# Spreading the denominators with 32-row tiles in a four-layer attention and MLP kernel

## The chip, the core and the metric

The kernel runs on one core of a Trainium2 chip. The metric is the device time of one execution in microseconds (us). The core has TensorE (PE in the profile, with its weight loads listed as PEld), VectorE (DVE), ScalarE (ACT), GpSimd (POOL) and SyncE (SP). Each works through its own queue of instructions in order and waits on semaphores for the others. TensorE writes its results to PSUM, which is divided into banks.

## The reference

Four layers run one after the other on x of 2048 rows and 576 columns, in bf16. Layers 1 and 3 are linear attention with 32 heads of 18 columns and share their weights; layers 2 and 4 are an MLP with 4608 hidden columns and share theirs. Each layer normalizes its input and adds its result to it.

```
def _A_ref(x, wqkv, wo):                       # layers 1 and 3
    qkv = x @ wqkv, split into q, k, v of 32 heads x 18
    phi = lambda t: where(t > 0, t + 1, exp(t)) + 1e-6
    pq, pk = phi(q), phi(k)
    kv  = einsum("bhsd,bhse->bhde", pk, v)     # 18 x 18 per head
    z   = einsum("bhsd->bhd", pk)
    num = einsum("bhqd,bhde->bhqe", pq, kv)
    den = einsum("bhqd,bhd->bhq", pq, z) + 1e-6
    return (num / den, heads side by side) @ wo

def _B_ref(x, w1, b1, w2, b2):                 # layers 2 and 4
    return gelu(layernorm(x) @ w1 + b1) @ w2 + b2

x = x + _A_ref(layernorm(x), ...)
x = x + _B_ref(layernorm(x), ...)
x = x + _A_ref(layernorm(x), ...)
x = x + _B_ref(layernorm(x), ...)
```

## The kernel before

Rows are handled in 16 tiles of 128, and tiles in 4 blocks of 512 rows (c is the block, j the tile within it, t = 4c + j). In the code a layer has the number li, from 0: attention is li = 0 and li = 2, called layer 1 and layer 3 here.

**An attention layer.** The first part makes keys, values and query projections and sums up the 18 x 18 matrices. `kv_wo` (L735) then multiplies each of five groups of heads with its rows of wo, so that the output of a row tile is five matmuls (one per group, 126 or 72 rows deep) for each half of the 576 columns. The queries, after phi, lie in tiles `pq[(g, c)]` with one head column per partition (7 heads x 18 = 126 partitions, 72 in group 4) and the 512 rows of the block along the free axis.

**The denominators.** For each block, `den_stage` (L750) has TensorE make the denominators of all 32 heads: for each of four column blocks of 128 rows, 32 heads on 32 partitions, in one PSUM tile of 128 x 128. ScalarE turns them into reciprocals as exp(-ln(den)), in the tile `rden`. They now have to be spread over the 18 columns of each head. `quad_stage` (L769) has VectorE place the four 32-partition strips of `rden` as a block diagonal into a 128 x 512 tile `quad_rden`, with a mask. `scale_stage` (L779), once per group, has TensorE multiply the selection matrix `head_bc[:, g, :]` with it (one matmul of 512 columns, 128 deep, L784), ScalarE copy the result out of PSUM to `rden_bc` (L788) and VectorE multiply `pq` with it in place (L789). With `direct=True` the copy is left out and VectorE reads PSUM.

**The output loop** runs over t from 0 to 15 (L834). `wo_stage(t)` (L793) is ten matmuls into one of two PSUM tiles, accA or accB by turns; `residual` (L504) adds the old row tile on VectorE and stores the sum to `x_d` through SP. In between come the work of the next block (its five scale stages after tiles 0 and 1 of this block, the den stage of the block after next after tile 1) and what is left of the query projections. The old row tiles come from `prefetch_xo` (L486): pairs straight from the input in layer 1, and row tiles from `x_d` in layer 3. They share the pool `rows`, nine tiles, with the sums; a tile is free again when its last reader or store is done. `AHEAD` is 4.

**The next layer's normalization.** `lnp` (L301) is a pipeline whose items move by one step on each `tick`: statistics, rstd, mean times rstd, normalized rows, transposes on TensorE with a copy to `yT`. In the output loop it takes the first four row tiles for the MLP; `hold` is the number of ticks that an item waits first, `tp_at` the tile t from which its transposes may go. Statistics are made on VectorE, or, with `stats="act"`, by two passes on ScalarE that are put behind the last reciprocal.

**PSUM.** The pool `ps_h` has four banks, used in turn by query projections (until phi has read them on ScalarE), den stages, scale stages and transposes. `ps_acc` holds accA and accB of two banks each.

**Order.** Within the attention layers and the MLP, `pe()` chains TensorE's instructions in the order of the code. On the other engines a planner orders instructions when the kernel is built, by the order of the code and by when it reckons that they are ready; dependencies of the kind NOSYNC (`tc.add_manual_dep`) force an order where they stand.

**The start.** All first loads go through SP in one chain (`chained`): row tiles 0 and 1, the key part of wqkv, row tile 2, the value part, and so on. ScalarE loads its table of functions at once.

Of the kernel before, what the change touches and what calls it, by code (L numbers as in the profile page):

```python
# [8 lines left out]
ALU = mybir.AluOpType  # L9
BF16 = mybir.dt.bfloat16  # L10
F32 = mybir.dt.float32
# [4 lines left out]
P = 128  # L16
NT = S // P
# [11 lines left out]
CA = 512  # L29
NCA = S // CA  # L30
# [4 lines left out]
def build(tc, A_x, A_wqkv, A_wo, B_w1, B_b1, B_w2, B_b2, out, dbg=None, n_layers=4):  # L35
    nc = tc.nc
    dbg = dbg or {}
    with ExitStack() as ctx:
        const = ctx.enter_context(tc.tile_pool(name="const", bufs=1))
        ps_h = ctx.enter_context(tc.tile_pool(name="ps_h", bufs=4, space=PSUM))  # L40
# [3 lines left out]
        x_in = A_x.flatten_outer_dims()  # L44
# [14 lines left out]
        head_bc = const.tile([P, G, P], BF16, name="head_bc")  # L59
# [49 lines left out]
        AHEAD = 4  # L109
        turned = const.tile([P, D // 32, TPC, 32], BF16, name="turned")  # L110
# [6 lines left out]
        rows = ctx.enter_context(tc.tile_pool(name="rows", bufs=9))  # L117
# [6 lines left out]
        NOSYNC = mybir.DependencyInfo(mybir.DependencyClass.NoSync, mybir.DependencyReason.SCHED_ONLY)  # L124
# [3 lines left out]
        chain = dict(last=None)  # L128

        def chained(inst):  # L130
            if chain["last"] is not None:
                tc.add_manual_dep(inst.ins, chain["last"], NOSYNC, reason="start-up DMA issue order")
            chain["last"] = inst.ins.name
            return inst
# [3 lines left out]
        def pe(inst):  # L138
            if pe_chain["on"]:
                if pe_chain["last"] is not None:  # L140
                    tc.add_manual_dep(inst.ins, pe_chain["last"], NOSYNC, reason="TensorE order in the MLP")
                pe_chain["last"] = inst.ins.name
            return inst

        def load_x0(t):
            x0 = blk.tile([P, D], BF16, name="x0", tag="blk")
            chained(nc.sync.dma_start(out=x0[:], in_=x_in[t * P:(t + 1) * P, :]))
            x0_tiles[t] = x0

        def load_wqkv(part):  # L150
# [3 lines left out]
            chained(nc.sync.dma_start(out=wqkv_sb[0:64, 4, cols], in_=A_wqkv[4 * P:D, cols]))  # L154

        load_x0(0)
        load_x0(1)
        load_wqkv(1)
        load_x0(2)
        load_wqkv(2)  # L160
        load_x0(3)
        load_x0(4)
# [10 lines left out]
                pe(nc.tensor.matmul(warm_ps[:], lhsT=y_ring[NY - 1][:, 0:P], rhs=y_ring[NY - 1][:, 0:512],  # L173
                                    start=True, stop=True))

        nc.scalar.preload_act_table_set("natural_log_exp_and_others")
        nc.vector.memset(wqkv_sb[64:P, 4, :], 0.0)
        for vr in v_ring:
            nc.gpsimd.memset(vr[:, 4, 72:126], 0.0)
# [40 lines left out]
        dve_last = dict(norm=None, sum=None, phi=None)  # L220
# [223 lines left out]
        lnp = LNPipe()  # L444
# [41 lines left out]
        def prefetch_xo(li, t, add_b2):  # L486
            if li == 0:
                if t % 2 == 0:
                    pair = rows.tile([P, 2, D], BF16, name="xo_pair", tag="row")
                    chained(nc.sync.dma_start(  # L490
                        out=pair[:], in_=x_in[t * P:(t + 2) * P, :].rearrange("(two p) d -> p two d", two=2)))
                    for i in range(2):
                        xo_of[(li, t + i)] = pair[:, i, :]
                return
            xo = row_tile("xo")
            load = nc.sync.dma_start(out=xo[:], in_=x_d[t])
            if not add_b2:
                behind(load, "landed")
            if add_b2:
                tc.add_manual_dep(load.ins, dve_last["sum"], NOSYNC, reason="no residual rows ahead of their stage")  # L500
                nc.gpsimd.tensor_tensor(out=xo[:], in0=xo[:], in1=b2_bc[:], op=ALU.add)  # L501
            xo_of[(li, t)] = xo[:]
# [25 lines left out]
        def layer_A(li, next_kind, pre_a1=None):  # L528
# [217 lines left out]

            quad_rden = {}
            rden_of = {}

            def den_stage(c, after=None, pair=None):  # L750
                if pair:
                    dp = ps_acc.tile([P, 2, 512], F32, name="den_pair", tag=pair)[:, 0, :]
                else:
                    dp = ps_h.tile([P, 512], F32, name="den_ps", tag="h")
                for g in range(G):
                    rows = 127 if g == 0 else GR[g]
                    for j in range(TPC):
                        pe(nc.tensor.matmul(dp[32 * j:32 * (j + 1), 0:P], lhsT=zsel[0:rows, g, :],
                                         rhs=pq[(g, c)][0:rows, j * P:(j + 1) * P],
                                         start=(g == 0), stop=(g == G - 1)))  # L760
                rden = work.tile([P, P], BF16, name="rden", bufs=1)
                log = nc.scalar.activation(out=dp[:, P:2 * P], in_=dp[:, 0:P], func=ACT.Ln)
                if after is not None:
                    tc.add_manual_dep(log.ins, after, NOSYNC, reason="copies first")
                act_last["rden"] = nc.scalar.activation(out=rden[:], in_=dp[:, P:2 * P], func=ACT.Exp,
                                                        scale=-1.0).ins.name
                rden_of[c] = rden

            def quad_stage(c, after=None):  # L769
                quad = blk.tile([P, D], BF16, name="quad_rden", tag="blk")  # L770
                spread_out = nc.vector.tensor_tensor(
                    out=quad[:, 0:CA].rearrange("p (j n) -> p j n", j=4), in0=quad_mask[:],
                    in1=rden_of.pop(c)[:].unsqueeze(1).to_broadcast([P, 4, P]), op=ALU.mult)
                if after is not None:
                    tc.add_manual_dep(spread_out.ins, after, NOSYNC, reason="sums first")
                quad_rden[c] = quad
                dve_last["quad"] = spread_out.ins.name

            def scale_stage(g, c, pair=None, direct=False):  # L779
                if pair:  # L780
                    bp = ps_acc.tile([P, 2, 512], F32, name="rden_pair", tag=pair)[:, 0, :]
                else:
                    bp = ps_h.tile([P, 512], F32, name="rden_ps", tag="h")
                pe(nc.tensor.matmul(bp[:, 0:CA], lhsT=head_bc[:, g, :], rhs=quad_rden[c][:, 0:CA], start=True, stop=True))  # L784
                spread_rows = bp
                if not direct:
                    spread_rows = blk.tile([P, D], BF16, name="rden_bc", tag="blk")
                    act_last["copy"] = nc.scalar.copy(out=spread_rows[0:GR[g], 0:CA], in_=bp[0:GR[g], :]).ins.name  # L788
                mult = nc.vector.tensor_tensor(out=pq[(g, c)][0:GR[g], 0:CA], in0=pq[(g, c)][0:GR[g], 0:CA],  # L789
                                               in1=spread_rows[0:GR[g], 0:CA], op=ALU.mult)  # L790
                dve_last["mult"] = mult.ins.name

            def wo_stage(t):  # L793
                c, j = divmod(t, TPC)
                wp = ps_acc.tile([P, 2, 512], F32, name="wo_ps", tag=("accA", "accB")[t % 2])
                for half in range(2):
                    for g in range(G):
                        pe(nc.tensor.matmul(wp[:, half, 0:HALF], lhsT=pq[(g, c)][0:GR[g], j * P:(j + 1) * P],  # L798
                                              rhs=kvwo[g][0:GR[g], half * HALF:(half + 1) * HALF],
                                              start=(g == 0), stop=(g == G - 1)))  # L800
                xn = residual(li, t, wp[:, :, 0:HALF])
                if xn is not None and next_kind == "B" and t < TPC:
                    lnp.feed(xn, t, "B", "pool", "act", hold=(2, 2, 6, 6)[t], tp_at=6 + 2 * t,
                             **(dict(after="sum") if t % 2 else dict(stats="act", after="rden")))

            for t in range(AHEAD):
                prefetch_xo(li, t, add_b2=False)
            if "b1" in bias_stage:
                bias_casts()
# [12 lines left out]
            if li == 0:  # L822
                late = [q_proj(*q_left.pop(0), defer=True)]
            for g in range(3):
                scale_stage(g, 0)
            kv_wo(4)
            scale_stage(3, 0, pair="accA")
            late.append(q_proj(*q_left.pop(0), defer=True))
# [4 lines left out]
                phi(after=act_last["rden"])  # L833
            for t in range(NT):  # L834
                c, j = divmod(t, TPC)
                if t + AHEAD < NT:
                    prefetch_xo(li, t + AHEAD, add_b2=False)
                wo_stage(t)
                for late in list(rden_of):
                    quad_stage(late, after=dve_last["sum"])  # L840
                if q_left:
                    q_proj(*q_left.pop(0))
                if c + 1 < NCA:
                    for g in ((0, 1, 2), (3, 4), (), ())[j]:
                        scale_stage(g, c + 1)
                if j == 1 and c + 2 < NCA:
                    den_stage(c + 2)
                if t == NT - 3:
                    warm_table(ACT.Gelu_apprx_tanh, act_last["copy"])
                state["wo"] = t  # L850
                lnp.tick()
                if t < 10:
                    lnp.tick(transposes=0)
# [237 lines left out]
```

## Time and profile before

| | |
|---|---|
| median of 3 runs | 766.43 us (766.31 to 766.50) |
| the profiled execution | 766.11 us, of which its span is 764.4 us |
| granted TensorE clock | 1.000 |
| TensorE busy | 758.8 us, 6522 matmuls |
| ScalarE, VectorE, GpSimd busy | 336.5, 271.6, 123.4 us |
| layer 1, output stage | about 77 to 106 us of the span |
| layer 3, output stage | about 453 to 479 us of the span |

The profile is of one execution. Its times run from the first instruction. In a line of the timeline stand the start, the length, the engine, the line of the code (L784), the operation, what it writes and reads, the shapes, the number of instructions merged (x3), and in brackets the idle time of that engine just before, with what ended it. Groups carry busy time, mean ns of one, and idle time before. SPq is SyncE's queue of transfers.

### The profile page before, as it was taken

What the parts mean: (1) busy time and instruction counts of PE and PEld (TensorE: products, weight loads), DVE (VectorE), ACT (ScalarE), POOL (GpSimd) and SP (SyncE); (2) the same over time, 40 slices, a digit from 0 to 9 for tenths busy, and PEclk for the clock granted to TensorE, in tenths of its full rate; (3) what the DMA queues carried; (4) which work ended last, traced back from release to release, by engine and by line L of the source; (5) the groups of instructions that cost most, each with busy time, mean ns of one, the idle gap of its engine ahead of it and who ended that gap; (6) DMA issues with size and microseconds to landing.
All of it is one profiled execution on the core that took longest, in us unless ns stands there. A gap on an engine that the chain in (4) does not pass through costs nothing.

```text
span 764.4 us, 15650 instructions
## 1 busy us (share of the span) xinstructions
PE 758.8 (99%) x6522; PEld 492.1 (64%) x6522; DVE 271.6 (36%) x684; ACT 336.5 (44%) x751; POOL 123.4 (16%) x198
## 2 busy tenths in 40 slices
PE   8999999999999999999999999999999999999998
PEld 6776664675477457646777767447745764674476
DVE  7785963135113603400355678600240032000000
ACT  5888856304710650164056577570064036205600
POOL 4681222012000301200110004200020021001000
PEclk9999999999999999999999999999999999999999
DMA  9992473016401721330246007530231033011000
GB/s 262 270 299 49 158 275 85 17 47 178 110 24 63 203 62 42 97 85 1 75 120 215 1 16 245 206 81 17 62 105 41 16 125 81 9 32 55 2 9 24
DMA packets 80289, 73.82 MB, mean 97 GB/s; under 512 B 36698, under 2 KB 64858, under 8 KB 80218
## 3 DMA queue, kind: packets, MB, share of 16 engines
q1 hardware_dynamic: 80218, 72.82, 32.6%
q8 instruction: 51, 0.84, 0.5%
q14 instruction: 20, 0.16, 0.1%
HBM read 48.03 MB, written 24.77 MB: 95 GB/s over the span
## 4 chain that ended last, share of the span: by engine, by line
PE 98%; DVE 1%; DMA 1%; ACT 0%; SPq 0%; issue 0%
PE m_ps L972 36%; PE h_ps L914 20%; PE hp_ps L914 16%; PE q_ps L588 5%; PE wo_ps L798 5%; PE k_ps L540 3%; PE k_ps L612 3%; PE k_ps L629 2%; PE v_ps L561 1%; PE m_half L972 1%; PE v_ps L558 1%; PE rden_ps L784 1%; PE tp L423 1%; DMA wqkv_sb<-in_A_wqkv_dram 1%; PE kvacc L582 1%; PE k_tail L629 1%
## 5 line engine op out<-in xcount | busy, mean ns | idle before, releaser
L972 PE MATMUL m_ps<-w_sb,hT 128*128 128x288 bf16 x2232 | 274.8, 286 | 0.0
L972 PEld LDWEIGHTS <-hT 128*128 128x128 bf16 x2304 | 224.8, 98 | 59.8 <-issue 3.4
L914 PEld LDWEIGHTS <-w_sb 64*128 64x128 bf16 x2304 | 124.5, 94 | 136.5 <-issue 1.9
L914 PE MATMUL hp_ps<-yT,w_sb 64*128 64x512 bf16 x1152 | 178.0, 376 | 0.0
L914 PE MATMUL h_ps<-yT,w_sb 64*128 64x512 bf16 x1152 | 148.0, 376 | 0.0
L919 ACT COPY relay_sb<-relay_sb 128x1 f32<-128x1 f32 x144 | 28.6, 198 | 262.3 <-PE h_ps L914 220.0
L910 ACT ACTIVATE hT<-h_ps,b1T 128x512 bf16<-128x512 f32 x144 | 91.2, 684 | 44.4 <-PE h_ps L914 44.4
L374 POOL TENSOR_TENSOR ln_rstd<-ln_u,neg_half 128x1 f32<-128x1 f32 x64 | 36.6, 574 | 370.8 <-DVE ln_u L365 226.4
L910 ACT ACTIVATE hT<-hp_ps,b1T 128x512 bf16<-128x512 f32 x144 | 91.2, 693 | 0.0
L518 DVE TENSOR_TENSOR xbf<-m_ps,xo 128x576 bf16<-128x576 f32 x15 | 11.4, 757 | 212.9 <-PE m_ps L972 212.9
L518 DVE TENSOR_TENSOR xo<-m_ps,xo 128x576 f32<-128x576 f32 x16 | 12.1, 758 | 176.1 <-PE m_ps L972 176.1
L501 POOL TENSOR_TENSOR xo<-xo,b_bc 128x576 f32<-128x576 f32 x32 | 41.0, 1287 | 100.4 <-DMA xo<-x_d 63.7
L914 PE MATMUL h_ps<-yT,w_tail 64*128 64x512 bf16 x144 | 54.1, 376 | 0.0
L914 PE MATMUL hp_ps<-yT,w_tail 64*128 64x512 bf16 x144 | 54.1, 376 | 0.0
L588 PE MATMUL q_ps<-yT,wqkv_sb 128*126 128x512 bf16 (+1 forms) x200 | 49.8, 380 | 0.0
L798 PE MATMUL wo_ps<-kvwo,pq 126*128 126x288 bf16 (+1 forms) x320 | 43.3, 286 | 0.5 <-DVE pq L789 0.5
L914 PEld LDWEIGHTS <-w_tail 64*128 64x128 bf16 x288 | 27.1, 94 | 17.1
L798 PEld LDWEIGHTS <-pq 126*128 126x128 bf16 (+1 forms) x320 | 30.1, 97 | 10.5 <-DVE pq L789 1.0
L467 ACT ACTIVATE phi_e<-k_ps 128x288 bf16<-128x288 f32 x46 | 19.3, 419 | 38.8 <-PE k_ps L612 35.8
L588 PEld LDWEIGHTS <-wqkv_sb 128*126 128x126 bf16 (+1 forms) x200 | 24.9, 131 | 11.4 <-issue 0.2
L475 DVE TENSOR_SCALAR phi_e<-phi_e 128x288 bf16<-128x288 bf16 (+2 forms) x86 | 24.7, 288 | 20.1 <-ACT phi_e L467 19.4
L467 ACT ACTIVATE phi_e<-q_ps 126x512 bf16<-126x512 f32 (+1 forms) x40 | 23.8, 596 | 18.0 <-PE q_ps L588 18.0
(136 smaller groups left out, 657.0 us busy)
## 6 DMA issues: line engine op xcount, KB each, us to landing
xo<-x_d SPq DMA_DIRECT2D x48, 288.0 KB
x_d<-xo SPq DMA_DIRECT2D x32, 288.0 KB
xl<-x_d SPq DMA_DIRECT2D x24, 288.0 KB
y_d<-turned SPq DMA_DIRECT2D x40, 144.0 KB
w_sb<-in_B_w_dram SPq DMA_DIRECT2D x6, 864.0 KB
yT<-y_d SPq DMA_DIRECT2D x10, 512.0 KB
w_sb<-in_B_w_dram SPq DMA_DIRECT2D x9, 512.0 KB
x_d<-xn SPq DMA_DIRECT2D x16, 288.0 KB
```

Of the source, the lines that this page charges most:

```text
L374: nc.gpsimd.tensor_tensor(out=rstd[:], in0=it["u"][:], in1=neg_half[:], op=ALU.pow)
L467: exp = nc.scalar.activation(out=e_out, in_=ps_ap, func=ACT.Exp)
L475: low = nc.vector.tensor_scalar(out=e[0:rows, 0:n], in0=e[0:rows, 0:n], scalar1=1.0, scalar2=1e-6, op0=ALU.min, op1=ALU.add)
L501: nc.gpsimd.tensor_tensor(out=xo[:], in0=xo[:], in1=b2_bc[:], op=ALU.add)
L518: total = nc.vector.tensor_tensor(out=xn[:, cols].rearrange("p (h n) -> p h n", h=2), in0=halves, in1=xo[:, cols].rearrange("p (h n) -> p ...
L588: pe(nc.tensor.matmul(qp[0:GR[g], :], lhsT=wqkv_sb[:, k, GO[g]:GO[g] + GR[g]], rhs=yT[:, k, c * CA:(c + 1) * CA], start=(k == 0), stop=(k ...
L629: pe(nc.tensor.matmul(dst, lhsT=lhsT, rhs=pk, start=(t == 0), stop=(t == NT - 1)))
L798: pe(nc.tensor.matmul(wp[:, half, 0:HALF], lhsT=pq[(g, c)][0:GR[g], j * P:(j + 1) * P], rhs=kvwo[g][0:GR[g], half * HALF:(half + 1) * HALF ...
L910: act_last["gelu"] = nc.scalar.activation(out=to, in_=ps, func=ACT.Gelu_apprx_tanh, bias=b1T[:, f:f + 1], scale=1.0).ins.name
L914: mm = pe(nc.tensor.matmul(dst[n], lhsT=wt, rhs=mv, start=(seen[n] == 0), stop=(seen[n] == 8)))
L919: relay = nc.scalar.copy(out=relay_sb[:, 1:2], in_=relay_sb[:, 0:1])
L972: pe(nc.tensor.matmul(acc[half][:, 0:HALF], lhsT=hT[f][:, j * P:(j + 1) * P], rhs=w2_sb[:, f, half * HALF:(half + 1) * HALF], start=(f == ...
```

## The change

In both attention layers the spread of blocks 1 to 3 is made another way. `quarter_stage(c)` needs no block diagonal for groups 0 to 3: for each group and each 32-partition strip i of `rden` it makes one matmul 32 rows deep, 126 wide, of 128 columns, which fits in a 32-row tile of the array. The four strips write four different PSUM banks, all of `ps_h`, each of which in the end holds the four groups of one strip. ScalarE copies the four banks to `turned`, a tile that otherwise serves to turn rows in the MLP, and `quarter_scale` has VectorE multiply the four groups from there. Group 4 still goes by `quad_stage` and `scale_stage`, and so does block 0.

The steps stand at other places in the loop: for block 1, the quarter stage comes after tile 1 and the products after tile 2; for block 2, the quarter stage comes after tile 3 and the products after tiles 4 and 5, and for block 3 after tile 7 and after tiles 8 and 9. Group 4 of block 1 is spread after tile 2, that of blocks 2 and 3 after tiles 4 and 8. The den stage of block 2 moves to tile 2. Query projections that are left go after tiles 0 and 2. Layer 3 asks for six residual row tiles before the loop instead of four. Layer 1's group 0 of block 0 is multiplied straight from PSUM. The normalization items get other holds and transposition times and change statistics engines (even tiles on VectorE, odd ones on ScalarE). At the start, row tiles 1 and 2 are loaded through ScalarE's queue, ahead of its table.

```diff
-        def load_x0(t):
+        def load_x0(t, by_act=False):
             x0 = blk.tile([P, D], BF16, name="x0", tag="blk")
-            chained(nc.sync.dma_start(out=x0[:], in_=x_in[t * P:(t + 1) * P, :]))
+            if by_act:
+                chain["act"] = nc.scalar.dma_start(out=x0[:], in_=x_in[t * P:(t + 1) * P, :]).ins.name
+            else:
+                chained(nc.sync.dma_start(out=x0[:], in_=x_in[t * P:(t + 1) * P, :]))
...
-        load_x0(1)
+        load_x0(1, by_act=True)
         load_wqkv(1)
-        load_x0(2)
+        load_x0(2, by_act=True)
...
-        nc.scalar.preload_act_table_set("natural_log_exp_and_others")
+        load = nc.scalar.preload_act_table_set("natural_log_exp_and_others")
+        tc.add_manual_dep(load.ins, chain["act"], NOSYNC, reason="first rows first")
...
+            def quarter_stage(c):
+                rden = rden_now["tile"]
+                banks = [ps_h.tile([P, 512], F32, name="rden_ps", tag="h") for _ in range(4)]
+                for g in range(4):
+                    for i in range(4):
+                        rows = slice(32 * i, 32 * (i + 1))
+                        pe(nc.tensor.matmul(banks[i][0:126, g * P:(g + 1) * P], lhsT=head_bc[rows, g, 0:126],
+                                            rhs=rden[rows, :], start=True, stop=True))
+                spread_rows = turned[:].rearrange("p a t c -> p (a t c)").rearrange("p (i w) -> p i w", i=4)
+                for i in range(4):
+                    act_last["copy"] = nc.scalar.copy(out=spread_rows[0:126, i, 0:4 * P], in_=banks[i][0:126, :]).ins.name
+
+            def quarter_scale(c, groups, after):
+                spread_rows = turned[:].rearrange("p a t c -> p (a t c)").rearrange("p (i w) -> p i w", i=4)
+                for g in groups:
+                    scaled = pq[(g, c)][0:126, 0:CA].rearrange("p (i n) -> p i n", i=4)
+                    mult = nc.vector.tensor_tensor(out=scaled, in0=scaled,
+                                                   in1=spread_rows[0:126, :, g * P:(g + 1) * P], op=ALU.mult)
+                    tc.add_manual_dep(mult.ins, after, NOSYNC, reason="sums first")
+                    dve_last["mult"] = mult.ins.name
...
-                    lnp.feed(xn, t, "B", "pool", "act", hold=(2, 2, 6, 6)[t], tp_at=6 + 2 * t,
-                             **(dict(after="sum") if t % 2 else dict(stats="act", after="rden")))
-
-            for t in range(AHEAD):
+                    lnp.feed(xn, t, "B", "pool", "act", hold=(2, 2, 2, 4)[t] if li > 0 else (2, 8, 8, 10)[t], tp_at=6 + 2 * t if li > 0 else (6, 10, 11, 14)[t],
+                             **(dict(after="sum") if t % 2 == 0 else dict(stats="act", after="rden")))
+
+            for t in range(AHEAD if li == 0 else AHEAD + 2):
                 prefetch_xo(li, t, add_b2=False)
...
             for g in range(3):
-                scale_stage(g, 0)
+                scale_stage(g, 0, direct=(li == 0 and g == 0))
...
             for t in range(NT):
                 c, j = divmod(t, TPC)
-                if t + AHEAD < NT:
-                    prefetch_xo(li, t + AHEAD, add_b2=False)
+                if li == 0 and t + AHEAD < NT or 0 < t < NT - AHEAD - 1 and li > 0:
+                    prefetch_xo(li, t + AHEAD + (li > 0), add_b2=False)
                 wo_stage(t)
-                for late in list(rden_of):
-                    quad_stage(late, after=dve_last["sum"])
-                if q_left:
+                total = dve_last["sum"]
+                if c + 1 < NCA:
+                    for g in ((), (), (0, 1, 2, 3), ())[j] if c == 0 else ((0, 1), (2, 3), (), ())[j]:
+                        quarter_scale(c + 1, (g,), after=total)
+                    if t == 1:
+                        quarter_stage(1)
+                    if j == 3 and c + 2 < NCA:
+                        quarter_stage(c + 2)
+                    if j == (2 if c == 0 else 0):
+                        scale_stage(4, c + 1)
+                if j == (2 if c == 0 else 1) and c + 2 < NCA:
+                    den_stage(c + 2)
+                    if c > 0:
+                        quad_stage(c + 2, after=total)
+                if t == 3:
+                    quad_stage(2, after=total)
+                if q_left and t in (0, 2):
                     q_proj(*q_left.pop(0))
-                if c + 1 < NCA:
-                    for g in ((0, 1, 2), (3, 4), (), ())[j]:
-                        scale_stage(g, c + 1)
-                if j == 1 and c + 2 < NCA:
-                    den_stage(c + 2)
+                    if t == 2:
+                        q_proj(*q_left.pop(0))
```

## The prediction

> **What bounds the kernel now.** All times are in us. I read the page first: busy time and the chain of work that ended last.
>
> ```profile
> PE 758.8 (99%) x6522; PEld 492.1 (64%) x6522; DVE 271.6 (36%) x684; ACT 336.5 (44%) x751; POOL 123.4 (16%) x198
> ...
> PE 98%; DVE 1%; DMA 1%; ACT 0%; SPq 0%; issue 0%
> ```
>
> TensorE is the bound, so an edit counts only if it removes TensorE work, removes one of its few waits, or adds a wait. Next the TensorE timeline of layer 1's output stage (start, length; lengths overlap, so work is read from start to start).
>
> ```profile
> 77.08 0.67 PE L798 MATMUL wo_ps<-kvwo,pq 126*128 126x288 bf16 x4
> 78.02 0.91 PE L798 MATMUL wo_ps<-kvwo,pq 72*128 72x288 bf16 x6 [0.28 <-DVE pq L789]
> ...
> 82.81 0.59 PE L784 MATMUL rden_ps<-quad_rden,head_bc 128*128 128x512 bf16 x2
> 83.34 0.47 PE L758 MATMUL den_ps<-pq,zsel 127*32 127x128 bf16 x20
> 83.74 1.40 PE L798 MATMUL wo_ps<-kvwo,pq 126*128 126x288 bf16 x10
> ```
>
> Three things are read here. A wo tile costs 1.23 (ten matmuls). A spread matmul (L784) costs 0.216. The den stage, whose 20 matmuls go four abreast in 32-column tiles, occupies 83.74 - (82.81 + 2 x 0.216) = 0.50, and its single starts in the trace show why: 0.093 lost entering the tiled form, five steps of 0.045 to 0.057, 0.097 lost leaving. Then the one real wait, at layer 1's entry, on the engines that feed it:
>
> ```profile
> 74.64 1.57 ACT L788 CAST rden_bc<-rden_ps 126x512 bf16<-126x512 f32 x3
> 75.28 0.42 DVE L789 TENSOR_TENSOR pq<-pq,rden_bc 126x512 bf16<-126x512 bf16 x1 [1.13 <-ACT rden_bc L788]
> 75.62 0.75 DVE L743 CAST kvwo<-kvwo_ps 72x576 bf16<-72x576 f32 x1
> 76.28 1.08 DVE L789 TENSOR_TENSOR pq<-pq,rden_bc 126x512 bf16<-126x512 bf16 x3
> 77.29 0.68 DVE L789 TENSOR_TENSOR pq<-pq,rden_ps 72x512 bf16<-72x512 bf16 x1
> ```
>
> VectorE sat idle 1.13 for ScalarE's first copy; its last product ends at 77.97 and TensorE goes on at 78.02. The start of the kernel:
>
> ```profile
> 0.80 0.86 SPq L147 DMA_DIRECT2D x<-in_A_x_dram  x2
> 1.71 0.43 SPq L152 DMA_DIRECT2D wqkv_sb<-in_A_wqkv_dram  x1
> 5.80 0.48 ACT L426 COPY yT<-tp 128x384 bf16<-128x384 bf16 x1 [3.72 <-PE tp L423]
> 6.92 0.77 PE L540 MATMUL k_ps<-wqkv_sb,yT 128*128 128x288 bf16 x5 [0.61 <-DMA wqkv_sb<-in_A_wqkv_dram]
> ```
>
> **First loads.** Each issue holds SP for 0.43 to 0.47. With row tile 1 moved to ScalarE's queue, the key weights are issued 0.47 earlier (1.24 for 1.71). Against it, row tiles 0 to 2 (144 KB each) now land beside them; at the page's 262 GB/s one is 0.55. The first projection can start no earlier than the yT copy's end, 6.28. So the gain is between -0.1 and 0.6; I take 0.3, nearer the issue time, since the trace's packets are sparse around 3 to 4 us. On ScalarE two issues (0.9) go ahead of the table load (1.28, from 0.79): it ends near 3.0, before the first copy at 5.80. TensorE has no wait over 0.04 between 8.6 and 66, so the gain is carried on.
>
> **Layer 1's entry.** Group 0's product now reads PSUM: 0.68 on VectorE instead of 0.42, but it can start when the spread ends (74.44), not at 75.28. ScalarE loses one copy (0.48). The four later products then end about 0.5 earlier, and TensorE's 0.44 before 78.02 shrinks to under 0.1. A wait of 0.12 before the query projection at 75.29, for a bank that the copy frees, goes too. Gain 0.5; bounds 0.2 and 0.57. What is late next is TensorE itself.
>
> **The quarter spread.** For blocks 1 to 3 of each layer, four spread matmuls (4 x 0.216 = 0.864) become sixteen of 128 columns, four abreast in 32-row tiles. No row shows 32-row tiles. The nearest is the den stage: the same two changes of form (0.19) and steps of four 128-column matmuls; here four steps, not five. Its weights are 32 wide, these 126; a 126-wide load in L649 of layer 3 holds a 0.057 step:
>
> ```profile
> 447.32 0.96 PE L649 MATMUL kv_ps<-k,wqkv_sb 128*126 128x126 bf16 x15
> ```
>
> So 0.19 + 4 x 0.057 = 0.42, and I take 0.45, as a first wide load after a change of form costs up to 0.05 more in that stage (0.105 for 0.057). The ends are 0.35 (part of the change hidden) and 1.10 (loads one by one). Saving 0.41 x 6 = 2.5. By the Trainium skill, TensorE: Matmul & The Clock Gate, Measured speedup vs the span model, 4x row packing was measured at 3.07 times; by that the four steps would take 0.864 / 3.07 = 0.28 (an estimate) instead of 0.23 and the sum would be 0.3 smaller; no run here shows it yet.
>
> ScalarE still makes four copies and VectorE four products per block, of the same sizes:
>
> ```profile
> L788 ACT CAST rden_bc<-rden_ps 126x512 bf16<-126x512 f32 x30 | 15.9, 597 | 5.2 <-PE rden_ps L784 5.2
> L789 DVE TENSOR_TENSOR pq<-pq,rden_bc 126x512 bf16<-126x512 bf16 x32 | 13.3, 437 | 1.9 <-ACT rden_bc L788 1.3
> ```
>
> **The new wait.** The quarter stage takes all four banks of ps_h, so its first four matmuls wait for the last user of each, and everything behind in TensorE's order waits too. I laid the stage out by those rows' cadences (ScalarE 0.48 a pass, VectorE 0.33 a product and 0.66 a sum); the same layout of the kernel before ends each layer within 0.15 of the trace. Layer 1: block 1 is ready at about 80.5, but the last query tile's second pass ends near 80.66, 0.14; block 2 the same, behind two projections, 0.14; block 3 waits for a yT copy behind statistics on ScalarE, 0.23. Layer 3: 0.14, 0.05 and 0.23. There the group 4 spread of block 2, 1.23 (one wo tile) after the quarter stage, must get a bank back, while ScalarE has a row's two statistics passes (0.80 + 0.78) and the first copy (0.60) to do: 0.4. Together 1.3; ends 0.6 and 2.1.
>
> **Edits at nothing.** The residual tiles: the trace has nine loads issued in one go already,
>
> ```profile
> 404.67 4.96 SPq L496 DMA_DIRECT2D xo<-x_d  x9
> ```
>
> as many as the row pool has tiles, so loading six ahead instead of four moves none. Later loads wait for a tile on SP with the stores x_d behind; their cover is time (the tenth tile's load goes out at 463.4, its sum starts at 471.1). If that is gone, VectorE's sum waits and, two tiles on, TensorE; the nearest row is the one sum in the list of waits that waited 1.0 for such a load. The statistics that change engine and place lie beside TensorE. Layer 1's last transposes move to t = 14, so their copy (0.44 + 0.72) has wo 15 and the switch to cover it (0.28 + 1.23): 0.3 to spare, and up to 0.3 if ScalarE is late.
>
> **Sum.** 0.3 + 0.5 + 2.5 - 1.3 = 2.0. The profiled execution took 766.11 (span 764.4 and 1.7 around it), so its like is 764.1; it lay 0.32 below the median 766.43, so I forecast 764.4. A run tells a change of about 0.2% (1.5 us) from none.
>
> **Rivals.**
> 1. The waits eat the saving: statistics passes are put ahead of the copies in both layers, so the third quarter stage of layer 1 waits 1.0 and not 0.23, and layer 3 loses another 0.5 in waits at wo 4 and at the next spread. For it: the statistics at 92.26 in the trace run ahead of a yT copy whose transpose had long ended. Against: these holds were moved, so the order may be another. Gain about 0.7: 765.7. Chance 0.22.
> 2. Slower: the sixteen weight loads go one after another. Then a step is 4 x 0.057, the stage 0.91 + 0.19 = 1.10, each of six loses 0.24 (1.4), and with waits of about 0.9 the sum is 0.3 + 0.5 - 1.4 - 0.9, 1.5 slower: 767.9. It decides from a stage of about 0.78 on. For it: no row here has four wide loads within one step. Against: L914's two 64-row loads start 0.004 apart and their matmuls run in pairs. Chance 0.12. The Trainium skill speaks for this one in part: LDWEIGHTS (loading the stationary operand), on the same page, has a load's time set by its columns, so that 32 rows cost as much as 128, and its 126 / 1.2 = 105 ns (an estimate) would make it dearer still; the 0.057 steps of L649 are against that figure.
> 3. The banks come free in time: waits of 0.3 and a stage of 0.40 give 0.3 + 0.5 + 2.8 - 0.3 = 3.3 faster: 763.1. Chance 0.08.
>
> **How the numbers follow.** The forecast's case has the remaining 0.58; its own range, from first loads (-0.3 to +0.3) and waits (0.6 to 2.1), is 763.2 to 765.5, and about a tenth of the chance lies above 764.9, the 0.2% mark. So faster: 0.47 + 0.08 = 0.55. Rival 2 straddles the mark on the other side (767.96), and a shortage of row tiles could add to it: slower 0.10. The rest is 0.35. The range 762.7 to 766.6 holds the forecast and rivals 1 and 3 with their bounds and leaves out rival 2.
>
> **What would show it.** Right: 96 matmuls of 32 rows, L784 down from 40 to 16, each quarter stage 0.40 to 0.50 from start to start; the wait before 78.02 gone; k_ps starting near 6.6; TensorE waits of 0.05 to 0.4 ahead of the quarter stages, released by ScalarE. Wrong: quarter stages near 1.1, or waits of 1 us in the output stages, or VectorE sums waiting for xo loads.

## The result and the profile after

| | before | after |
|---|---|---|
| median | 766.46 us (766.31 to 766.72, 6 runs) | 771.29 us (771.09 to 773.13, 6 runs) |
| ratio | | 1.0066, 95% interval 1.0056 to 1.0077 |
| profiled execution | 766.11, span 764.4 | 773.13, span 771.4 |
| granted TensorE clock | 1.000 | 0.995 |

The change makes the kernel 4.8 us slower; the forecast was 764.4, or 2.0 faster. The profile of after is of the slowest of its six executions; it lies 1.8 above the others. It loses 1.79 at the start, which only some executions do, as the runs on the first loads below show; that the other five are quicker there and nowhere else was not profiled. All times below are in us.

The page of after, busy time, chain, and the group of wo matmuls:

```profile
PE 761.1 (99%) x6594; PEld 492.7 (64%) x6594; DVE 271.4 (35%) x684; ACT 335.9 (44%) x750; POOL 125.2 (16%) x198
PE 95%; DVE 2%; DMA 1%; issue 0%; ACT 0%; SPq 0%; POOL 0%; DVEq 0%; ACTq 0%
L826 PE MATMUL wo_ps<-kvwo,pq 126*128 126x288 bf16 (+1 forms) x320 | 45.5, 291 | 4.9 <-DVE xo L522 4.8
```

TensorE's busy time should have fallen by the spread that went, and it is 2.3 longer; its share of the chain fell from 98% to 95%; and wo now waits 4.8 for VectorE's sums. In TensorE's timeline of layer 1, the parts that were forecast are there:

```profile
78.79 1.48 PE L826 MATMUL wo_ps<-kvwo,pq 126*128 126x288 bf16 x10
...
82.51 0.45 PE L806 MATMUL rden_ps<-rden,head_bc 32*126 32x128 bf16 x16
82.89 0.91 PE L826 MATMUL wo_ps<-kvwo,pq 126*128 126x288 bf16 x6
```

The ten wo matmuls at layer 1's entry run through without the wait of 0.44, and the quarter stage takes 0.38 from its first start to the next wo, with 0.096 lost ahead of it: 0.475, in all six places.

The account, by starts of TensorE's stages in the two profiles: the start loses 1.79 (den_ps of block 0 at 73.83 instead of 72.04), layer 1 from there to its first h_ps gains 1.57 (32.37 for 33.94), layer 2 and layer 3's first part change by nothing (the first den_ps of layer 3 comes at 447.15 instead of 446.93, the 0.22 that the first two leave), the output stage of layer 3 from its first wo to the MLP's first h_ps loses 5.62 (32.27 for 26.65), and what follows loses 1.18 (286.20 for 285.02).

The loss in layer 3 starts on SP. The list of its waits, for the load of a residual row tile (line L500 in after):

```profile
SPq L500 <- DMA x_d<-xo: 6.6, 3, 5.0
SPq L500 <- POOL y_ring L395: 4.6, 2, 3.3
```

(us in total, times, longest; in before the same two read 2.8, 3, 1.4 and 2.3, 1, 2.3.) Then the timeline of layer 3, in order:

```profile
466.36 1.82 POOL L395 TENSOR_SCALAR y_ring<-xo,ln_rstd,ln_nmr 128x576 bf16<-128x576 f32 x1
468.21 0.32 SPq L500 DMA_DIRECT2D xo<-x_d  x1
468.63 0.85 SPq L529 DMA_DIRECT2D x_d<-xo  x2
474.55 0.32 SPq L500 DMA_DIRECT2D xo<-x_d  x1
...
477.71 0.76 DVE L522 TENSOR_TENSOR xo<-wo_ps,xo 128x576 f32<-128x576 f32 x1 [2.75 <-DMA xo<-x_d]
478.53 1.39 PE L826 MATMUL wo_ps<-kvwo,pq 126*128 126x288 bf16 x10 [1.66 <-DVE xo L522]
...
481.92 1.48 DVE L522 TENSOR_TENSOR xo<-wo_ps,xo 128x576 f32<-128x576 f32 x2 [3.44 <-DMA xo<-x_d]
482.73 2.56 PE L826 MATMUL wo_ps<-kvwo,pq 126*128 126x288 bf16 x10 [2.81 <-DVE xo L522]
```

The load of row tile 11 is to go into the buffer of row tile 2, which GpSimd is still normalizing until 468.18; SP waits for it with that load at the head. Behind it in SP's queue stand the stores of sums 4 and 5; sum 4 was done by 464.4, but its store goes out at 468.63; sum 5 was done at 466.48, its store goes at 469.06. The load of row tile 12 is to go into the buffer of row tile 4, so it waits until that store has landed, at 474.53. In before the planner had the buffers in another order: the load of row tile 11 went into row tile 4's, behind that store (464.67), and did not wait for GpSimd. The loads of row tiles 11, 12 and 15 there, and the last three row tiles on TensorE:

```profile
467.81 0.32 SPq L496 DMA_DIRECT2D xo<-x_d  x1
...
470.09 0.32 SPq L496 DMA_DIRECT2D xo<-x_d  x1
...
473.96 0.45 SPq L496 DMA_DIRECT2D xo<-x_d  x1
...
475.58 3.86 PE L798 MATMUL wo_ps<-kvwo,pq 126*128 126x288 bf16 x30
```

So in before the loads of row tiles 12 to 15 had gone out at 470.09 to 473.96; after the change they go at 474.55 to 478.36, and the transfers then take 3.0 to 6.1 to land among the others. Sums 12 and 13 wait 2.75 and 3.44 for their rows, and TensorE, two PSUM tiles on, 1.82 and 2.98 (by its starts). What it does next is at half speed, as the table by stretches shows (the columns are length, busy time of each engine with its instructions, granted clock, DMA share, GB/s):

```profile
470.00:476.00 6.00, 6.00 (x58) 4.85 (x56) 4.42 (x9) 3.92 (x7) 0.98 (x2) 1.00 0.46 138
476.00:482.00 6.00, 2.26 (x18) 1.52 (x16) 0.84 (x2) 0.37 (x1) 0.00 (x0) 0.90 0.96 307
482.00:488.00 6.00, 5.27 (x26) 2.35 (x27) 2.16 (x3) 0.19 (x1) 0.00 (x0) 0.53 1.04 398
```

The granted clock is 0.53 in the last row, and wo matmuls go at steps of 0.240 instead of 0.122. The DMA share of 0.46 in the first row shows the stalled queue: in before it was 0.88 in the same stretch.

```profile
470.00:476.00 6.00, 6.00 (x55) 4.69 (x53) 4.67 (x9) 4.65 (x9) 2.23 (x4) 1.00 0.88 308
```

### The profile page after: what moved, and what is told of

It reads as the page before. It is cut to its first block, busy times and chain, and to the rows that moved or that the text cites. A ratio compares the mean times of both kernels' runs of the same rounds, so it can differ in the third digit from the quotient of the medians.

```text
span 771.4 us, 15788 instructions
## 1 busy us (share of the span) xinstructions
PE 761.1 (99%) x6594; PEld 492.7 (64%) x6594; DVE 271.4 (35%) x684; ACT 335.9 (44%) x750; POOL 125.2 (16%) x198
## 4 chain that ended last, share of the span: by engine, by line
PE 95%; DVE 2%; DMA 1%; issue 0%; ACT 0%; SPq 0%; POOL 0%; DVEq 0%; ACTq 0%
PE m_ps L1011 36%; PE h_ps L953 20%; PE hp_ps L953 16%; PE q_ps L592 6%; PE wo_ps L826 4%; PE k_ps L616 3%; PE k_ps L544 2%; PE k_ps L633 2%; PE v_ps L565 1%; PE m_half L1011 1%; PE v_ps L562 1%; PE tp L427 1%; DMA xo<-x_d 1%; DVE xo L522 1%; PE k_tail L633 1%; PE kvacc L586 1%
## 5 line engine op out<-in xcount | busy, mean ns | idle before, releaser
L826 PE MATMUL wo_ps<-kvwo,pq 126*128 126x288 bf16 (+1 forms) x320 | 45.5, 291 | 4.9 <-DVE xo L522 4.8
```

## The experiments

Theory A: the order on SP costs the time in layer 3. The first four runs set it against the six tiles ahead (B), the quarter spread or the normalization on other engines (C) and the shorter holds by themselves (D).

**Four tiles ahead.** The diff is against after.

```diff
-            for t in range(AHEAD if li == 0 else AHEAD + 2):
+            for t in range(AHEAD):
...
-                if li == 0 and t + AHEAD < NT or 0 < t < NT - AHEAD - 1 and li > 0:
-                    prefetch_xo(li, t + AHEAD + (li > 0), add_b2=False)
+                if t + AHEAD < NT:
+                    prefetch_xo(li, t + AHEAD, add_b2=False)
```

> After, with the residual tiles of layer 3 asked for as before (four at the entry, then one four tiles on at each row tile) instead of six and five on. Theory A (the queue order of layer 3 costs the time, and six or four tiles make no difference to it, since nine loads go out in one go in either): as after, 771.0 to 771.6, VectorE's sums waiting 2.7 and 3.4 for loads again. Theory B (asking two tiles further ahead fills the nine row tiles too early): the waits of layer 3 go, 764.5 to 766. The start's share: if den_ps of block 0 comes at 72.0 in this profile rather than at 73.8, the 1.8 that the profiled run of after lost at the start is chance of that run; if it is 73.8 again, it belongs to the change.

Measured: 770.57 (769.26 to 771.93, 4 runs), ratio 1.0054 (1.0039 to 1.0069). The program that is built from it has the same instructions in the same order on every engine as after: the planner sends nine loads out at once either way. So B falls, and the run is a second profile of after. In it TensorE waits 0.94 and 2.20 for late sums, and layer 3's output stage takes 29.87 where the first profile has 32.27, so the loss there differs between executions. den_ps of block 0 comes at 72.35: the 1.8 at the start is not in every execution.

**Stores first.** One order is added on SP; the order of the other four engines stays as in after.

```diff
+        last_store = {}
...
                 behind(load, "landed")
+                if t >= 9:
+                    tc.add_manual_dep(load.ins, last_store["ins"], NOSYNC, reason="stores first")
...
-            nc.sync.dma_start(out=x_d[t], in_=xn)
+            store = nc.sync.dma_start(out=x_d[t], in_=xn)
+            last_store["ins"] = store.ins.name
```

> After, with each residual load of layer 3 from the tenth tile on held in SP's order behind the store of the row tile summed before it; no other engine's order changes. Theory A (a load that waits on SP for POOL's normalization of row tile 2 keeps the stores of sums 4 and 5 behind it, and the next load takes the tile whose store was kept): the waits of VectorE's sums for loads (2.75 and 3.44) fall under 1.2 each, TensorE's 4.8 ahead of wo and the half-speed stretch behind them go, layer 3 ends at least as early as before: 764.3 to 766.0. Theory C (layer 3's quarter spread or its normalization on the other engines costs the time, and SP only follows): SP's stores go out earlier but TensorE's waits stay, 770 to 771.5.

Measured: 764.53 (764.36 to 766.06, 10 runs), ratio 0.9976 (0.9966 to 0.9985): 6.8 below after (6.0 below the same program in the run with four ahead) and 1.9 below before. SP's part of its timeline:

```profile
467.63 0.42 SPq L501 DMA_DIRECT2D xo<-x_d  x1
468.15 0.43 SPq L532 DMA_DIRECT2D x_d<-xo  x1
468.68 0.89 SPq L501 DMA_DIRECT2D xo<-x_d  x1
```

and TensorE's:

```profile
474.04 3.86 PE L830 MATMUL wo_ps<-kvwo,pq 126*128 126x288 bf16 x30
477.83 1.04 PE L957 MATMUL h_ps<-yT,w_sb 64*128 64x512 bf16 x8
```

The load of row tile 11 waits for GpSimd as in after (it goes out at 466.77, and all of this profile lies 1.44 earlier). But the store of sum 4 has gone out at 462.98, as the sum ended, so the load of row tile 12 follows at 467.63, where after has it at 474.55; the last load is out by 473.2, and thirty wo matmuls follow each other with no wait into the MLP. The output stage of layer 3 takes 26.32 instead of 32.27, and the granted clock is 1.00 throughout it. The loads of row tiles 11 and 12 take the same buffers as in after; nothing but the place of the loads in one queue was changed, so A is shown and C falls.

**Layer 3's normalization as before.**

```diff
-                    lnp.feed(xn, t, "B", "pool", "act", hold=(2, 2, 2, 4)[t] if li > 0 else (2, 8, 8, 10)[t], ...
-                             **(dict(after="sum") if t % 2 == 0 else dict(stats="act", after="rden")))
+                    lnp.feed(xn, t, "B", "pool", "act", hold=(2, 2, 6, 6)[t] if li > 0 else (2, 8, 8, 10)[t], ...
+                             **(dict(after="sum") if t % 2 == (li > 0) else dict(stats="act", after="rden")))
```

> After, with the normalization behind layer 3 as before: holds 2, 2, 6, 6 and ScalarE's statistics on row tiles 0 and 2 turned back to 1 and 3 as they were. Theory A: the order that the planner gives SP then has the stores of sums 4 and 5 ahead of the load that waits, so the time falls as in the run with stores first, 764.3 to 766.0. Theory C as the quarter spread itself: no change, 770 to 771.5. Theory D (the shorter holds bring POOL's and ScalarE's work against the sums, whatever SP does): this run falls to 764.3 to 766.0 and the one with stores first does not.

Measured: 765.44 (765.35 to 767.07, 10 runs), ratio 0.9995 (0.9986 to 1.0005). The loss goes as with the stores first: with this normalization the planner itself puts the stores of sums 4 and 5 ahead of the load of row tile 11. So the new normalization caused the order, and it cost time through SP; which part of it did, the holds or the exchanged statistics' engines, was not separated. In this loop it is not worse in itself: layer 3's output stage takes 27.14 here and 26.32 with the new normalization and the stores first.

**Before, with layer 3's normalization of after.**

```diff
-                    lnp.feed(xn, t, "B", "pool", "act", hold=(2, 2, 6, 6)[t], tp_at=6 + 2 * t,
-                             **(dict(after="sum") if t % 2 else dict(stats="act", after="rden")))
+                    lnp.feed(xn, t, "B", "pool", "act", hold=(2, 2, 2, 4)[t] if li > 0 else (2, 2, 6, 6)[t], tp_at=6 + 2 * t,
+                             **(dict(after="sum") if t % 2 == (li == 0) else dict(stats="act", after="rden")))
```

> Before, with only the normalization behind layer 3 as after has it (holds 2, 2, 2, 4, the statistics' engines exchanged). Its SP order has two loads in a row once, but the stores of sums 4 and 5 ahead of them. Theory A (what costs is the stores kept behind a waiting load, not the normalization): within 0.6 of before, 765.9 to 767.1. Theory D (the normalization's new holds cost it by themselves): slower by 3 to 6, 769.5 to 772.5.

Measured: 766.61 (766.15 to 767.02, 10 runs), ratio 1.0004 (0.9994 to 1.0014). D falls: in the old loop, where the stores of sums 4 and 5 stay ahead of the load of row tile 11, the new normalization costs 0.36 in layer 3 (27.01 for 26.65) and no stall.

**The first loads alone**, on before: the first hunk of the change (`by_act` for row tiles 1 and 2, and the table behind them).

> Before, with only the first loads as after has them (row tiles 1 and 2 on ScalarE's queue). The prediction's term was 0.3 faster, about 766.1. What the profiles of the changed kernels have since shown (row tile 0 lands at 3.67 to 3.71 instead of 2.99, the first tp at 6.1 instead of 5.4, den_ps of block 0 at 72.4 in two profiles and at 73.8 in two) says slower: 0.4 in most executions, 766.7 to 767.0, and 1.8 in some, 768.0 to 768.4. In the profile row tile 0 lands after 3.6 and TensorE waits 1.4 to 1.7 ahead of the first tp.

Measured: 766.58 (766.34 to 768.05, 11 runs), ratio 1.0012 (1.0002 to 1.0021). Seven executions lie at 766.34 to 766.65 and four at 767.82 to 768.05. Row tile 0 lands at 3.58 and the first tp starts at 6.01.

**Stores first, with the first loads of before.**

```diff
-        load_x0(1, by_act=True)
+        load_x0(1)
-        load_x0(2, by_act=True)
+        load_x0(2)
-        tc.add_manual_dep(load.ins, chain["act"], NOSYNC, reason="first rows first")
```

> The kernel with the stores first, with the first loads put back as before. If the first loads cost 0.4 to 1.8: median 763.9 to 764.2, no execution above 765, den_ps of block 0 near 72.0. If they gained 0.3 as forecast: 764.8. It keeps the quarter spread in both layers, layer 1's entry and the normalization of after, so its distance to before is what these are worth without the two losses: forecast 2.5 (quarter spread) plus 0.5 (entry) less waits.

Measured: 764.33 (763.79 to 764.76, 11 runs), ratio 0.9977 (0.9968 to 0.9985): the lowest median of the study, and one group only; by its ratio it cannot be told from the run with stores first alone (0.9976). den_ps of block 0 comes at 72.14.

**One load on ScalarE.**

```diff
-        load_x0(1, by_act=True)
+        load_x0(1)
```

> The kernel with the stores first, with only row tile 2 on ScalarE's queue and row tile 1 back on SP behind row tile 0. If it is row tile 1, issued in the same moment as row tile 0, that delays row tile 0: it lands near 3.0 again, first tp near 5.4, and the key part of wqkv is still issued 0.5 earlier than row tile 2 would let it: 763.6 to 764.2. If any load beside it delays row tile 0: as the kernel with stores first, 764.4 to 764.7 with some executions near 766.

Measured: 765.25 (764.53 to 766.24, 11 runs), ratio 0.9990 (0.9981 to 0.9999). Row tile 0 still lands at 3.67: ScalarE has nothing to issue first now and sends row tile 2 at 0.79, in the same moment as row tile 0. So it is not row tile 1 in particular; a second load issued in the same moment is enough. The edit did not make the load late as meant, and a later issue on ScalarE was not tried.

**Before, with the stores first.** The diff is that of the stores first.

> Before, with the same order of stores and loads on SP in layer 3 as the kernel with stores first. If the order is worth time by itself (the one sum that waited 1.0 for a load in before goes): 765.0 to 765.6, and a part of what the run with stores first gained over before is not the change's. If it only undoes what the change spoilt: 766.2 to 766.7.

Measured: 766.35 (766.05 to 766.75, 10 runs), ratio 1.0002 (0.9993 to 1.0011). The order is worth nothing by itself; it takes away what the change had added.

**Two more warming matmuls**, in the kernel with the stores first and the first loads of after.

```diff
-        warm_pe(9)
+        warm_pe(11)
```

> The kernel with the stores first and the first loads of after, with eleven warming matmuls ahead of the first row tile instead of nine (two at 0.43 cover 0.85 of the 0.97 that TensorE waits ahead of the first tp). Theory G (the 1.5 that some executions lose at the start comes from the idle stretch, after which TensorE runs at half speed): every execution falls into the quicker group, median 764.4, none above 765.3, and every k_ps of the profile takes steps of about 0.12 from the first. Theory H (the full speed is granted at a moment that has nothing to do with this stretch): the two groups stay, 764.4 and 766.0. If the two matmuls delay the first tp: 764.8 in the quicker group.

Measured: 764.59 (764.54 to 764.98, 10 runs), ratio 0.9978 (0.9968 to 0.9987). Ten executions lie within 0.44, where the same kernel with nine had two of ten near 766.05. At that share ten in a row without one would come by chance about once in nine times; over this kernel, the one with layer 3's normalization as before and the one with the first loads alone the slower group has 9 of 31, which makes it about once in thirty. So theory G is favoured over H. TensorE's start in after, and with eleven:

```profile
1.31 4.02 PE L176 MATMUL warm_ps<-y_ring 128*128 128x512 bf16 x9 [1.31 <-DVE y_ring L171]
6.10 0.71 PE L427 MATMUL tp<-ident,y_ring 128*128 128x128 bf16 x5 [0.76 <-DVE y_ring L399]
6.61 1.06 PE L176 MATMUL warm_ps<-y_ring 128*128 128x512 bf16 x2
```

```profile
1.31 4.87 PE L176 MATMUL warm_ps<-y_ring 128*128 128x512 bf16 x11 [1.31 <-DVE y_ring L171]
6.14 0.53 PE L427 MATMUL tp<-ident,y_ring 128*128 128x128 bf16 x5
6.51 0.59 PE L176 MATMUL warm_ps<-y_ring 128*128 128x512 bf16 x2
```

The two matmuls behind tp take 1.06 in after, behind an idle 0.76, and 0.59 with eleven, without it. In the profile of after, k_ps goes in steps of 0.240 until 9.85 and of 0.122 from there; with eleven it is at 0.122 to 0.133 from the first, one wait aside. But the idle stretch does not always cost this. In the run with four ahead, the same program as after, the two matmuls are quick behind the same 0.76:

```profile
6.38 0.60 PE L176 MATMUL warm_ps<-y_ring 128*128 128x512 bf16 x2
```

Of the six profiles with nine warming matmuls and a first load on ScalarE, three run k_ps at half speed until 9.8 to 10.8 (idle 0.76 to 0.79) and three do not (idle 0.76 to 1.32). The stretch is needed, as far as these runs show, and does not decide alone.

**No direct group 0**, in the kernel with the stores first and the first loads of before.

```diff
-                scale_stage(g, 0, direct=(li == 0 and g == 0))
+                scale_stage(g, 0)
```

> The kernel with the stores first and the first loads of before, without the direct scaling of group 0 at layer 1's entry. The prediction put layer 1's entry at 0.5 (0.2 to 0.57); in the profiles TensorE's wait there went from 0.44 to 0.06, so it should come back: the stretch from the first wo of layer 1 to its first h_ps 27.8 instead of 27.41, median 764.5 to 764.9. If the scaling is hidden with the quarter spread behind it: no change, 764.2 to 764.4.

Measured: 764.78 (764.34 to 765.47, 11 runs), ratio 0.9981 (0.9972 to 0.9990); the stretch from layer 1's first wo to its first h_ps is 27.79. The intervals of this run and of the one it is set against overlap, so the reading rests on the stretch and on the wait, which is back in the timeline:

```profile
78.32 0.91 PE L829 MATMUL wo_ps<-kvwo,pq 72*128 72x288 bf16 x6 [0.28 <-DVE pq L798]
```

## Why the prediction was wrong

**The residual tiles.** The step that failed is the one under "Edits at nothing". Its first half held: loading six ahead moves no load. Its second half named the path (a later load waits for a tile on SP with the stores behind it, the sum waits, TensorE waits two tiles on) and took the time between the tenth tile's load and its sum as cover. It treated the order on SP as fixed and the tiles' releases as those of before. But the holds and the statistics' engines had been moved too, booked at nothing since they lie beside TensorE; with them the planner's order on SP came out another, and a load that waits for GpSimd stood ahead of the stores whose buffers the next two loads needed. The price given, one wait of 1.0, was too small as well: 4.8 of waits on TensorE, and about 2.3 more at half speed behind them (layer 3 5.95 longer than with the stores first, and 1.17 after it, less the 4.80), 7.1 in the profiled execution. A shortage of row tiles had only a share in the 0.10 for slower, and should have been a rival of its own; the prediction's own signs of being wrong had it, as sums on VectorE that wait for xo loads.

**First loads.** Forecast 0.3 faster. Alone, on before, they are 0.3 slower in the quicker group (766.48 against 766.18) and 1.7 in the other (767.9). Between the two kernels with the stores first the quicker group shows no difference: with these loads it lies 1.9 below before in its own round, without them the median lies 1.85 below. The key part of wqkv did land earlier, 5.98 for 6.88, as the step said. What failed is "the first projection can start no earlier than the yT copy's end, 6.28", taken as fixed: with a second load issued in the same moment row tile 0 lands at 3.67 instead of 2.99, and carries the whole chain along (first tp at 6.10 instead of 5.42, the copy at 6.64 instead of 5.80, or at 6.47 where the clock was full). The bounds stopped at 0.1 on the side of a loss because they compared issue times with one transfer's size, and left out that TensorE can lose clock with a longer idle stretch.

**Layer 1's entry.** Forecast 0.5. The direct group is worth 0.38 between the first wo and h_ps (27.79 less 27.41) and 0.08 ahead of it (5.04 less 4.96 from den_ps to wo): 0.46.

**The quarter stage.** Forecast 0.45, measured 0.475, so 0.389 is saved six times, 2.3 for 2.5. The serial loads of rival 2 do not show: the sixteen matmuls start in four groups of four, 3 or 4 ns apart within a group, and from the last start of a group to the first of the next it is 0.095, 0.048 and 0.047. Less the 0.19 of the two changes of form, the four steps took 0.285, where the nearest row had said 0.23. The Trainium skill, TensorE: Matmul & The Clock Gate, Measured speedup vs the span model, had given 0.28 (an estimate, from a factor measured at 512 columns, where these have 128): the trace agrees with it in the sum. From group to group the starts show a first step of 0.105, then 0.058 and 0.057, as the first wide load in the prediction's L649 took 0.105 and the next ones 0.057; with that extra of 0.05 in full, the nearest row had 0.19 + 0.28 = 0.47.

**The new waits.** Forecast 1.3. In layer 1 there is none ahead of a quarter stage, and in layer 3 none either; what is left is 0.25 ahead of the group 4 spread of block 2 (0.4 was forecast), 0.09 within the wo before it, 0.46 ahead of a wo that waits for an earlier sum, all in layer 3, and 0.05 at a query projection in layer 1: 0.85 together. For the quarter stages the banks came free in time, as rival 3 had it. Rival 1 had two of the places in layer 3 right (wo 4 and the spread behind it, 0.34 for its 0.5), and its wait of 1.0 in layer 1 did not come.

**The sum without the two failures.** The kernel with the stores first and the first loads of before holds exactly the other three terms. By the prediction it should gain 0.5 + 2.5 - 1.3 = 1.7; by its parts 0.46 + 2.33 - 0.85 = 1.94; it gained 1.92 in the profile, from den_ps of block 0 to the end, and 1.85 in the median (766.18 to 764.33). So the entry and the quarter spread worked as forecast. That the waits came near is in part luck: the 0.93 forecast ahead of the quarter stages did not come, and the largest one that did come, 0.46, had not been named. The result was decided by two parts that the forecast had booked at nothing and at a small gain.

## What to carry to other kernels

When a change moves work that releases buffers, list which load waits for which reader on the in-order queue, and what stands behind that load, before booking the move at nothing: one load at the head of SP's queue held two finished stores for 4.2 and 2.6 us, and the next load needed one of these. A load that may wait belongs behind the stores that free the next buffers; that order alone was worth 6.0 to 6.8 us here, and nothing in before, whose loads went out in time as they stood. And a load issued in the same moment as the first one of this kernel delayed the first by 0.6 to 0.7 in every profile that has one, more than the 0.5 of issue time that it saved.

## What was not expected of the hardware

TensorE lost its full clock after waits that did not fill the stretch they lay in. In the second profile of after it waited 0.94 and 2.20 with 1.2 of work between; wo ran on at steps of 0.122 until 480.4 and went on at 0.240; the trace's record of the granted clock has half speed from 480.38 to 483.79, for 3.41. In the first profile it has half speed from 480.82 to 487.65, for 6.83 or twice 3.41. In the 3.4 ahead of either fall TensorE sat idle for about 2.2 and worked for the rest.

The Trainium skill, TensorE: Matmul & The Clock Gate, What's actually happening, has the clock fall after at least one idle window of about 3.4 us and rise after a busy one, on windows that run freely. The stretches of 3.41 and 6.83, and a loss at the start that comes and goes, fit such windows; that 2.2 of idle in one was enough does not fit a window that has to be idle throughout. At which share of work a window counts as busy was not measured.
